# TensorE order from a list scheduler, q and k turned by DMA, and a second bank for projection two: one change to a tuned attention and MLP kernel

## The chip, the cores and the metric

The kernel runs on one core of one Trainium2 chip. The metric is the device time of one execution in microseconds, as the median of several executions. Before the change it was 508.17 us (three runs, 508.09 to 509.68). A profile gives the span of one execution, about 2 us less than its time.

Ratios below are the mean time of one kernel's fast runs over the mean of the other's fast runs of the same rounds on the same chip, so they are not quite the ratio of the medians quoted beside them. A run counts as slow when it is over 1.5% above the fastest of the same kernel.

## The reference, cut to what matters

```python
# q, k, v: (8, 12, 448, 64) float32; w_in: (768, 2048); w_out: (2048, 768); tau = 0.1
q_n = q / (norm(q, axis=-1) + 1e-6)
k_n = k / (norm(k, axis=-1) + 1e-6)
attn = softmax(q_n @ k_n.T / tau)            # per batch and head, 448 x 448
x = (attn @ v).transpose(0, 2, 1, 3).reshape(8 * 448, 768)
h = x @ w_in                                 # projection one
out = (h * cos(h)) @ w_out                   # projection two
```

## The kernel before

A **pair** is two heads of one batch; there are 48 pairs, six to a batch. A **unit** is three pairs, and there are 16 units, numbered from 0. Within a pair TensorE does this: eight transposes of the scaled q and k (into the PSUM tile TP), eight score matmuls (into SC), then for the pair before it eight matmuls of the probabilities PX with v and eight with ones, which give the row sums (both into AV). After six pairs come the 96 matmuls of projection one for a whole batch (into SC and AV again), and 112 of projection two for each batch (into PO) are spread over the following pairs as filler.

Between the attention and projection one lies a chain of small steps for each unit: DVE or ACT copies AV to xu; four DMAs gather the row sums into sums; DVE adds and inverts them (rcp); one DMA writes them to DRAM (scr); two DMAs broadcast them (RB); and POOL multiplies xu by RB into xT, the input of projection one.

The program gives every engine a fixed list of instructions. In the kernel before, a small simulation with assumed durations orders the instructions of ACT, DVE, POOL and SP. TensorE's order, after the first batch, is the order in which the program text emits it, with projection two cut into portions by hand:

```python
    def pair(g, fa, fb):
        ...
        scores(g, 0)
        scores(g, 1)
        if g >= 1 and g != PB:
            attend(g - 1, direct(g - 1))
            if g % UP == 0:
                if g > PB:
                    chain(u - 1)
                ...
        m2_fill(fa)                       # fa, fb: so many matmuls of projection two
        ...
        if g + 1 < NG and g + 1 != PB:
            transposes(g + 1)             # eight on TensorE, then a DVE copy qkT <- TP
        scores(g, 2)
        scores(g, 3)
        m2_fill(fb)

    points = {PB * (b + 1) + (4 if b == 1 else 3): b for b in range(1, B - 1)}
    for g in range(PB, NG):
        ...
        pair(g, fa, fb)
        if g in points:
            m1(points[g])                 # projection one of batch b, after pair 3 or 4 of the next batch
            m2_fill(16)
            m2_add(points[g])
```

Projection two has one PSUM bank, so each run of 16 matmuls must wait until DVE has copied the last one out (from 130 us on TensorE waited four times for this, 3.5 us in all):

```python
    PO = ps("PO", [128, 512], F32)
    banks = [[("PO", PO.ap())]]
```

Of the kernel before, what the change touches and what calls it, by code (L numbers as in the profile page):

```python
# [19 lines left out]

class Op:
    __slots__ = ("eng", "fn", "idx", "deps", "cost", "mode", "dma", "bulk", "lock", "label", "bias",
# [3 lines left out]
class Program:  # L26

# [8 lines left out]
    PATIENCE = 0.25  # L36

    def __init__(self, new_sem):
        self.new_sem = new_sem
        self.ops = []  # L40
        self.writer = {}
        self.readers = {}
        self.free = False
        self.filler = None

    def op(self, eng, fn, reads=(), writes=(), cost=0.0, mode=None, dma=None, bulk=0.0, lock=False, label="", bias=0.0):
        o = Op()
        o.eng, o.fn, o.dma, o.cost, o.mode, o.bulk, o.lock = eng, fn, dma, cost, mode, bulk, lock
        o.label, o.idx, o.inc, o.count, o.late, o.bias, o.free = label, len(self.ops), False, None, None, bias, self.free
        deps = {}  # L50
# [30 lines left out]
    def arrange(self, passes=3):  # L81
        ops = self.ops
        nominal, t = {}, 0.0
        for o in ops:
            if o.eng == "PE":
                nominal[o.idx] = t
                t += o.cost * (1.1 if o.free else 1.0)
        fixed = {o.idx: nominal[o.idx] + 8.0 for o in ops if o.free and o.eng == "PE"}
        for n in range(passes):
            late = [1e9] * len(ops)  # L90
            for o in reversed(ops):
                if o.eng == "PE":
                    late[o.idx] = min(late[o.idx], nominal[o.idx])
                if late[o.idx] > 1e8:
                    late[o.idx] = nominal[max(nominal)] + 10.0
                took = o.cost + (2.2 + o.bulk if o.dma is not None else 0.0)
                for y, _ in o.deps:
                    ty = y.cost + (2.2 + y.bulk if y.dma is not None else 0.0)
                    v = late[o.idx] - ty - self.latency(y, o)
# [4 lines left out]
            self.play()  # L104
            nominal = {o.idx: fixed.get(o.idx, o.start) for o in ops if o.eng == "PE"}
        return self

    def play(self):
        ops = self.ops
        left = [len(o.deps) for o in ops]  # L110
        ready_at = [0.0] * len(ops)
        users = [[] for _ in ops]
# [8 lines left out]
        pe = [o for o in ops if o.eng == "PE"]  # L121
        waiting = {e: [] for e in self.ENGINES}
        for o in ops:
            if left[o.idx] == 0:
                waiting[o.eng].append(o)
        todo = len(ops)
        while todo:
            best = None
            for e in self.ENGINES:
                if e == "PE":  # L130
                    s = None
                    for o in pe[: self.WINDOW if pe and pe[0].free else 1]:
                        if o.free != pe[0].free:
                            break
                        if left[o.idx] == 0:
                            t = max(free[e], ready_at[o.idx])
                            if s is None or t < s - self.PATIENCE:
                                s, c = t, (t, 0, o)
                    if s is None:
                        continue  # L140
                else:
# [4 lines left out]
                    o = min((o for o in waiting[e] if ready_at[o.idx] <= now + 1e-9), key=lambda o: (o.late, o.idx))  # L146
                    s = now
                    if o.lock and e != "SP":
                        s = max(s, port)
                    c = (s, 1, o)  # L150
                if best is None or c[:2] < best[:2]:
                    best = c
            s, _, o = best
            e = o.eng
            if e == "PE":
                pe.remove(o)
# [12 lines left out]
            if o.dma is not None:  # L169
                o.end = max(o.end + 1.7, o.start + 2.2)  # L170
                if o.bulk:
                    server = max(server, o.start + 1.2) + o.bulk
                    o.end = max(o.end, server + 1.2)
                elif server > o.start:
                    o.end += 0.8
            for w in users[o.idx]:
# [6 lines left out]
                if left[w.idx] == 0:  # L183
# [101 lines left out]
def bass_cosine_attention__then__act_gcu_kernel(  # L285
# [13 lines left out]
    UP = 3  # L299
# [10 lines left out]
    RING = 2 * S  # L310
# [541 lines left out]
```

## Time and profile before

| before | value |
|---|---|
| time | 508.17 us |
| span of the profiled run | 506.3 us |
| TensorE busy, and idle (span less busy) | 471.5 and 34.8 us |
| next busiest engine | ACT, 285.1 us |
| bytes moved by DMA | 55.42 MB |

The prediction shows the main views. The groups of instructions add the two that the change removes or reshapes. The columns are line, engine, operation, output and inputs, tiling and shapes, count, then busy time and mean duration of one in ns, then the idle time just before:

```profile
L508 PE MATMUL TP<-ident,qks 112*128 112x112 bf16 x384 | 27.9, 216 | 4.8 <-POOL qks L491 4.0 <-DVE qks L491 0.8
L539 PE MATMUL AV<-PX,va 112*64 112x448 bf16 x384 | 47.7, 368 | 4.2 <-ACT xu L565 2.2 <-DVE gT L635 1.0 <-DMA va<-in_v_dram 0.5
```

All 384 transposes run on the busiest engine, and the AV product uses column tiles of 64 where the sums use 32.

### The profile page before, as it was taken

Reading aid. Unit: us, or ns where it says so; the run is one execution under the profiler, and the core shown is the slowest. Engines: PE = TensorE matmul, PEld = TensorE weight load, DVE = VectorE, ACT = ScalarE, POOL = GpSimd, SP = SyncE. Lnnn points to the kernel's source line nnn. Section 1 sums busy time; section 2 is a strip of 40 time slices with the busy share of each in tenths; the row PEclk is TensorE's granted clock in tenths of the full one; section 3 lists DMA queues with packets and bytes.
Section 4 is the critical chain, followed back from the end, with each engine's and each line's share of the span. In section 5 each row is a group of like instructions: output and inputs, shape, how many; then the busy total and the mean of one; then the engine's idle time right before and its main releaser. Section 6 shows DMA issues by size and latency. Waiting matters only on the chain.

```text
span 506.3 us, 7822 instructions
## 1 busy us (share of the span) xinstructions
PE 471.5 (93%) x3268; PEld 226.4 (45%) x3268; DVE 223.6 (44%) x286; ACT 285.1 (56%) x347; POOL 234.3 (46%) x162
## 2 busy tenths in 40 slices
PE   8988878988999899999799999999999999999996
PEld 3333333433444445444354444444554445454553
DVE  5644544255573445435363536435343233422521
ACT  4983375877556554777237655567557654641410
POOL 4926907749977672463724864267224022002000
PEclk9999787998999999999799999999999999999999
DMA  9995692977724672186502593064501622114012
GB/s 226 178 224 141 99 236 52 209 155 195 136 60 137 156 165 56 32 170 168 114 1 86 117 220 91 5 146 113 105 6 32 120 63 54 32 35 117 1 41 85
DMA packets 51650, 55.42 MB, mean 109 GB/s; under 512 B 8864, under 2 KB 46240, under 8 KB 51616
## 3 DMA queue, kind: packets, MB, share of 16 engines
q1 hardware_dynamic: 18848, 26.61, 19.8%
q0 software_dynamic: 16256, 11.80, 16.3%
q10 hardware_dynamic: 16512, 16.52, 13.0%
q8 instruction: 26, 0.43, 0.4%
q14 instruction: 8, 0.07, 0.0%
HBM read 55.25 MB, written 11.16 MB: 131 GB/s over the span
## 4 chain that ended last, share of the span: by engine, by line
PE 59%; DMA 20%; POOL 8%; issue 5%; DVE 3%; ACT 2%; SPq 1%; POOLq 0%; ACTq 0%
PE PO L676 17%; PE SC L619 15%; DMA raw<-in_q_dram 9%; PE AV L619 8%; PE SC L525 5%; PE AV L539 5%; POOL sq L465 4%; DMA va<-in_v_dram 3%; DMA RB<-scr 3%; DMA sums<-xu 3%; PE AV L547 3%; POOL xT L605 2%; PE TP L508 2%; PE SC L676 2%; POOL qks L491 2%
## 5 line engine op out<-in xcount | busy, mean ns | idle before, releaser
L530 ACT ACTIVATE PX<-SC 112x896 bf16<-112x896 f32 x192 | 165.2, 917 | 69.7 <-PE SC L525 67.0
L676 PE MATMUL PO<-W,gT 128*128 128x384 bf16 x752 | 137.7, 330 | 3.8 <-DVE osb L688 3.5
L491 POOL TENSOR_TENSOR qks<-raw,rn 112x1024 bf16<-112x1024 f32 x47 | 88.6, 1903 | 59.4 <-ACT rn L483 46.5
L619 PE MATMUL SC<-xT,W 128*128 128x448 bf16 x480 | 100.7, 367 | 6.5 <-POOL xT L605 4.9
L676 PEld LDWEIGHTS PO<-W,gT 128*128 128x128 bf16 x752 | 68.2, 98 | 71.6 <-issue 22.1
L465 POOL TENSOR_TENSOR sq<-raw 112x1024 bf16<-112x1024 f32 x43 | 80.4, 1891 | 38.3 <-DMA raw<-in_q_dram 38.3
L605 POOL TENSOR_TENSOR xT<-xu,RB 128x448 bf16<-128x448 f32 x42 | 46.4, 1133 | 108.2 <-DMA RB<-scr 108.2
L633 ACT ACTIVATE cosb<-SC,cst 128x896 f32<-128x896 f32 x40 | 40.2, 1007 | 73.6 <-PE SC L619 73.5
L619 PEld LDWEIGHTS SC<-xT,W 128*128 128x128 bf16 x480 | 47.7, 101 | 56.2 <-issue 11.3
L472 DVE TENSOR_REDUCE n<-sq 112x16 f32<-112x1024 bf16 (+1 forms) x49 | 58.0, 1189 | 29.4 <-POOL sq L465 23.9
L525 PE MATMUL SC<-qkT 64*128 64x448 bf16 x384 | 59.7, 365 | 9.1 <-DVE qkT L516 5.2
L635 DVE TENSOR_TENSOR gT<-SC,cosb 128x896 bf16<-128x896 f32 x40 | 43.5, 1090 | 50.4 <-ACT cosb L633 50.3
L619 PE MATMUL AV<-xT,W 128*128 128x448 bf16 x288 | 58.5, 352 | 0.7
L539 PE MATMUL AV<-PX,va 112*64 112x448 bf16 x384 | 47.7, 368 | 4.2 <-ACT xu L565 2.2
L688 DVE COPY osb<-PO 128x384 f32<-128x384 f32 x47 | 25.9, 552 | 56.9 <-PE PO L676 56.7
L516 DVE COPY qkT<-TP 128x896 bf16<-128x896 bf16 x48 | 29.5, 615 | 30.9 <-PE TP L508 30.9
L633 ACT ACTIVATE cosb<-AV,cst 128x896 f32<-128x896 f32 x24 | 24.2, 1008 | 31.0 <-PE AV L619 30.0
L619 PEld LDWEIGHTS AV<-xT,W 128*128 128x128 bf16 x288 | 27.7, 98 | 28.7 <-issue 3.6
L568 DVE COPY xu<-AV 128x896 f32<-128x896 f32 x21 | 22.9, 1091 | 35.6 <-PE AV L547 35.6
L635 DVE TENSOR_TENSOR gT<-AV,cosb 128x896 bf16<-128x896 f32 x24 | 26.2, 1090 | 22.2 <-ACT cosb L633 21.9
L508 PE MATMUL TP<-ident,qks 112*128 112x112 bf16 x384 | 27.9, 216 | 4.8 <-POOL qks L491 4.0
L525 PEld LDWEIGHTS SC<-qkT 64*128 64x128 bf16 x384 | 14.4, 94 | 39.6 <-ACT PX L530 17.4
(40 smaller groups left out, 246.1 us busy)
## 6 DMA issues: line engine op xcount, KB each, us to landing
RB<-scr SPq DMA_DIRECT2D x28, 336.0 KB, 4.6
raw<-in_k_dram ACTq DMA_DIRECT2D x12, 672.0 KB, 5.9
raw<-in_q_dram ACTq DMA_DIRECT2D x12, 672.0 KB, 8.8
va<-in_v_dram POOLq DMA_DIRECT2D x16, 336.0 KB, 5.7
W<-in_moe_w_in_dram POOLq DMA_DIRECT2D x4, 768.0 KB, 13.4
W<-in_moe_w_out_dram POOLq DMA_DIRECT2D x4, 768.0 KB, 10.8
out_dram<-osb SPq DMA_DIRECT2D x8, 336.0 KB, 2.8
out_dram<-osb SPq DMA_DIRECT2D x8, 288.0 KB, 2.6
```

The source lines that it names most:

```text
L465: pool(lambda e, x=x, y=y: e.tensor_tensor(y, x, x, ALU.mult), src_, dst, 0.1 + n * 1.78e-3, label="sq%d.%d" % (u, p))
L472: dve(lambda e, w=w: e.tensor_reduce(out=n2v[i][:, 2 * p : 2 * p + 2, w], in_=sqv[p][:, :, w, :], axis=mybir.AxisListType.X, op=ALU.add), ...
L491: f = lambda e, s0=s0, s1=s1: e.tensor_tensor(qksv[i][:, s0:s1, h, :].rearrange("p s h d -> p h s d"), rawv[i][:, h, s0:s1, :], bass.AP(rn ...
L508: r = e.transpose(TP.ap()[:, NP * s : NP * s + NP], qksv[i][:, s, 2 * p : 2 * p + 2, :], ident.ap())
L525: t = e.matmul(SCv[z][:, a, 0:S], qkT[j].ap()[r, NP * c : NP * c + 128], qkT[j].ap()[r, S : 2 * S], start=True, stop=True)
L530: act(lambda e: e.activation(PXv[j][:, c], SCv[z][0:NP, :, 0:S], ACT.Exp, scale=1.0 / TAU), ["SC%d" % z], [("PX", j, c)], 2 * S, "E", labe ...
L539: t = e.matmul(AVv[64 * a : 64 * a + 64, 0, 0:S], vav[i][:, NJ * (2 * p + a) + c, :], PXv[j][:, c, a, :], start=(c == 0), stop=(c == NJ - 1))
L605: pool(lambda e, p=p: e.tensor_tensor(xTv[b % 2][:, UP * i + p, :], xuv[i][:, 0, p, :], RBv[i][:, p, :], ALU.mult), [("RB", i, p), ("xu", ...
L619: t = e.matmul(ph[:, a, 0:S], W1v[:, c, 128 * n : 128 * n + 128], xTv[b % 2][:, c, :], start=(c == 0), stop=(c == NKC - 1))
L633: act(lambda e, ph=ph, cz=cz: e.activation(cosv[cz], ph[:, :, 0:S], ACT.Sin, bias=cst.ap()[:, 0:1], scale=1.0), names(gi) + ["cst0"], [("c ...
L635: dve(lambda e, ph=ph, cz=cz, gi=gi: e.tensor_tensor(gTv[:, 2 * gi : 2 * gi + 2, S * (b % 2) : S * (b % 2) + S], ph[:, :, 0:S], cosv[cz], ...
L676: r = e.matmul(po[:, 0:HW], gTv[:, y, col : col + 128], W2v[:, y, HW * hf : HW * hf + HW], start=(y == 0), stop=(y == NF - 1))
```

## The change

Its intent is to take work off TensorE and to let it find something to do whenever one stream waits. It has four parts.

**Part 1.** From pair 10 on (number 9, counted from 0), q and k are turned by a DMA, asked for two pairs ahead, into three buffers:

```diff
     def transposes(g, apart=False):
-        u, p, j = g // UP, g % UP, g % 2
+        u, p, j = g // UP, g % UP, g % 3
+        if g >= BYPE:                              # BYPE = 9
+            dma("SP", [lambda e: e.dma_start_transpose(
+                qkT[j].ap().rearrange("p (s m) -> p s m", s=NS), qksv[i][:, p].rearrange("p s h d -> p (s h d)"))],
+                ...
+            P.ops[-1].cost = 1.2
+            return
```

**Part 2.** The AV product is cut into four column tiles of 32, the form that the sums have. (The sums of the first six pairs, 48 matmuls in tiles of 64, take that form too.)

```diff
         def av(e, c):
             for a in range(2):
-                t = e.matmul(AVv[64 * a : 64 * a + 64, 0, 0:S], vav[i][:, NJ * (2 * p + a) + c, :], PXv[j][:, c, a, :], ...)
+                for h in range(2):
+                    o = 64 * a + 32 * h
+                    t = e.matmul(AVv[o : o + 32, 0, 0:S], vav[i][:, NJ * (2 * p + a) + c, 32 * h : 32 * h + 32], ...)
```

**Part 3.** The transposes' bank becomes a second bank of projection two once the transposes on TensorE are done:

```diff
-    TP = ps("TP", [128, 1024], BF16)
+    PO2 = ps("PO2", [128, 512], F32)
+    TPv = PO2.ap().bitcast(BF16)
...
+    banks[0] = [("PO", PO.ap()), ("PO2", PO2.ap())]
```

**Part 4.** The list scheduler now chooses TensorE's order too, from two streams: the attention with projection one (A), and projection two (B). It repeats with landing times of DMAs from a model of three queues, which it takes to share the DMA engines. Weight loads at the start are chained behind one another, and projection one of a batch is offered after pair 5 of the next batch. The orders of the other engines are made anew with the same model, and one squaring step of unit 3 moves from POOL to ACT. Part 4 is thus a bundle:

```diff
+            for grp in groups[:3]:
+                t = when(grp)
+                if t is not None and (s is None or switched(t, grp[0]) < s - self.PATIENCE):
+                    s, c = switched(t, grp[0]), (t, grp[0], grp)
+            if fill and left[fill[0].idx] == 0:
+                o = fill[0]
+                t = max(free["PE"], ready_at[o.idx])
+                if s is None or switched(t, o) < s - self.HOLD:
+                    s, c = t, (t, o, fill)
...
-    points = {PB * (b + 1) + (4 if b == 1 else 3): b for b in range(1, B - 1)}
+    points = {PB * (b + 1) + 5: b for b in range(1, B - 1)}
```

## The prediction

> **What bounds the kernel now.** I read four views in this order: the page's busy line and its 40 slices, the busy time by stretch, TensorE's timeline in one steady stretch, and TensorE's own waits. The busy line and three rows of the slices come first:
>
> ```profile
> PE 471.5 (93%) x3268; PEld 226.4 (45%) x3268; DVE 223.6 (44%) x286; ACT 285.1 (56%) x347; POOL 234.3 (46%) x162
> PE   8988878988999899999799999999999999999996
> PEclk9999787998999999999799999999999999999999
> DMA  9995692977724672186502593064501622114012
> ```
>
> TensorE is the bound: 93% busy, and no other engine is above 56%. So time falls only if TensorE gets less work, fewer gaps, or fewer stretches at a low granted clock. The slices say where the weak places are: in the first quarter PE is at 8, the clock dips to 7 and 8, and the DMA row is at 9 in many slices. The windows view (columns: stretch, its length, busy time of PE, PEld, DVE, ACT and POOL, granted clock, DMA share, GB/s), cut at the start and end of the first projection (41, 68) and where the second one begins (130):
>
> ```profile
> 0.00:41.00 41.00, 35.85 (x255) 15.02 (x255) 21.78 (x32) 30.10 (x48) 21.37 (x21) 1.00 1.07 215
> 41.00:68.00 27.00, 23.09 (x111) 10.82 (x108) 15.21 (x14) 9.02 (x11) 20.54 (x14) 0.87 0.63 120
> 68.00:130.00 62.00, 51.71 (x421) 21.16 (x420) 27.36 (x38) 47.44 (x62) 40.67 (x27) 0.89 0.72 157
> 130.00:244.00 114.00, 107.17 (x768) 52.51 (x768) 55.03 (x68) 67.19 (x79) 69.45 (x45) 1.00 0.53 122
> 244.00:461.00 217.00, 214.10 (x1496) 105.20 (x1497) 90.50 (x118) 121.97 (x140) 78.92 (x55) 0.99 0.36 81
> ```
>
> From 130 us on, TensorE is nearly full at full clock; there only removed work and a few gaps can help. Before 130 us it is 111 busy of 130, 16.5 us of that is filler on the zero tile (the group PO<-zt, 68 matmuls), and from 41 to 130 the clock is 0.87 to 0.89. What one steady pair of heads costs is in the timeline (start, length, group):
>
> ```profile
> 271.61 0.56 PE L508 MATMUL TP<-ident,qks 112*128 112x112 bf16 x8
> 272.10 0.55 PE L525 MATMUL SC<-qkT 64*128 64x448 bf16 x4
> 272.58 1.47 PE L676 MATMUL PO<-W,gT 128*128 128x384 bf16 x8
> 273.99 0.66 PE L525 MATMUL SC<-qkT 64*128 64x448 bf16 x4
> 274.57 0.95 PE L539 MATMUL AV<-PX,va 112*64 112x448 bf16 x8
> 275.45 0.56 PE L547 MATMUL AV<-PX,ones 112*32 112x448 bf16 x8
> 275.95 1.47 PE L676 MATMUL PO<-W,gT 128*128 128x384 bf16 x8
> 277.26 0.56 PE L508 MATMUL TP<-ident,qks 112*128 112x112 bf16 x8
> ```
>
> Ends are modelled, so I use start to start. The eight transposes hold TensorE 272.10 - 271.61 = 0.49 us. A block of eight second-projection matmuls takes 273.99 - 272.58 = 1.41 before a block in another tiling (64*128) and 277.26 - 275.95 = 1.31 before one in the same tiling: a tiling switch costs 0.10 us. One pair is 5.65 us, of which 2.72 is projection two. TensorE's gaps from 130 us on, in the view of waits, are few:
>
> ```profile
> PE SC L619 <- POOL xT L605: 4.9, 2, 3.7
> PE PO L676 <- DVE osb L688: 3.5, 4, 1.5
> ```
>
> The 3.7 us gap is at 240.7 us, and what follows it in the timeline is dearer than it should be:
>
> ```profile
> 244.47 7.55 PE L619 MATMUL SC<-xT,W 128*128 128x448 bf16 x24 [3.72 <-POOL xT L605]
> 254.13 4.70 PE L619 MATMUL SC<-xT,W 128*128 128x448 bf16 x24
> ```
>
> The same 24 matmuls take 2.85 us more after the gap.
>
> [...] 112 x 1024 elements of 2 bytes are 0.23 MB[...]. [...] the load of q issued at 61.55 us, with weights of projection two in flight, holds 17.5 us of the chain that ended last, where the median issue to landing of such loads is 8.8.
>
> **Part 1, transposes.** Pairs 9 to 47, thus 39 of 48, get q and k turned by a DMA on the SP queue, asked for two pairs ahead, into three buffers instead of two. Removed on TensorE: 39 x 0.49 = 19.1 us, all on the bounding engine. Removed on DVE: 39 copies qkT<-TP of 0.615 us = 24 us, off the path. Added: 39 x 0.23 MB = 9 MB of DMA[...]. Two pairs of lead is about 10 us. The kernel's own cost constant for the issue is 1.2 us of SP; even if landing takes 5 us it is hidden, provided that SP isn't stuck behind another wait. The SP queue is idle mostly.
>
> **Part 2, AV in four column tiles of 32 rather than two of 64.** The number of AV matmuls doubles to 768, but four run beside each other, so array time stays. What goes is the switch between AV (112*64) and the sums (112*32): one per pair, 48 x 0.10 = 4.8 us. Risk: twice the weight loads and instructions in the same 0.88 us. The sums block already runs eight matmuls of that form in 0.50 us including a switch, so sixteen should fit in about 0.80. I count no loss.
>
> **Part 3, second bank for projection two.** The transposes' bank is free after the first nine pairs. Removes the wait on the copy osb, 3.5 us from 130 us on.
>
> **Part 4, the order.** Projection two becomes a stream that fills whenever the attention stream isn't ready, and each projection one comes after the whole of the next batch's pairs, so that its last xT has long landed. Removes from 130 us on the 3.7 us gap, the 2.85 us of low clock after it, and about 1 us before AV: 7.6 us. I charge it for finer cuts (one more switch per pair, 31 x 0.10 = 3 us) and for wrongly foreseen waits in TensorE's fixed order (I choose 7 us, some 0.2 us a pair).
>
> **From 130 us on:** 376.3 us now, minus 30 transposes blocks x 0.49 = 14.7, minus 31 x 0.10 = 3.1, minus 3.5, minus 7.6, plus 10 = 357.
>
> **Before 130 us** three bounds compete. (a) Needed TensorE work at full clock: 17 pairs x 2.44 (5.65 less 2.72 and 0.49) = 41.5, nine transposes 4.4, projection one 18.2, ten blocks of projection two 13 to 14, longer sums of the first six pairs 2.3: 80, plus about 11 before the first scores = 91. (b) DMA: the DMA view moves 21.8 MB up to 130 us; at the 215 GB/s of the first 41 us that is 101 us. (c) POOL: 82.6 us busy plus a 10 us start = 93. DMA is the highest, and it was slack for long (0.63 and 0.72 from 41 to 130). The change reorders weight loads for this: the first weights wait for the first pairs, and half of projection two's weights come before the loads of the fourth unit. I take 12 us over the highest bound: 113, a saving of 17.
>
> **Sum:** 113 + 357 = 470, minus nothing for the tail, which keeps its last 4 us. The time is 508.2 against a span of 506.3, so add 2: 472. That includes my cautious 10 us of charges; a good fit of the schedule would give 462. I predict **467 us**.
>
> **The rivals.** (1) A new wait takes the old work's place: the DMA transposes land late, because SP issues in order and stands behind a gather, a spread or an output[...]. For it: SP waits 190 us in all for the copies osb, in its own view of waits, and SP's order was drawn from a model. Against it: 10 us of lead and a third buffer. If each of 39 pairs lost 1 us, the gain of part 1 is gone twice over: 467 + 39 = 506, the same. (2) The start is held by DMA whatever the order: the first 130 us remain, less the 3 us of transposes there: 127 + 357 + 2 = 486. For it: a DMA row at 9 in the early slices, and 9 MB more traffic, though little of it early. (3) ACT becomes the bound in the pair stretches: four exps x 0.917 = 3.67, half an xu 0.46, together 4.1 us a pair against TensorE's 5.65 - 0.49 - 0.10 = 5.06. Against it: TensorE is still longer. It would show as waits of scores on exp, filled by projection two until that runs dry; perhaps 0.3 us a pair, 480. (4) The scheduler does as well as it believes and the start falls to its bound: 101 + 347 + 2 = 450.
>
> **Range and chances.** Removed work alone, 19.1 + 4.8 = 24 us, gives 484 with no gap closed; to fail a 2% gain (498) most of it would have to return as waits. Rivals 2 and 3 together make about 490, rival 4 makes 450. So 448 to 490 at 8 in 10; faster by over 2% 0.92, within 2% 0.06, slower 0.02.
>
> **What would show it right or wrong.** TP matmuls fall from 384 to 72; AV<-PX,va shows 768 in the form 112*32 and its block, with the sums, takes about 1.28 us with no switch between. PE busy falls by some 25 to 35 us, with its share at 94% or more. The wait of PO on osb vanishes. The clock stays 1.00 after 130 us. M2 blocks fill gaps of the scores. Part 1 is wrong if the waits view lists PE or PEld SC on DMA qkT for more than about 5 us; the start's step is wrong if the second projection one does not begin at least 10 us earlier for the same pairs done; part 2 is wrong if an AV block of sixteen takes over 0.9 us. The whole is wrong if TensorE's share falls below 90%, as then its fixed order met waits that the scheduler did not see.

The sum: 113 + 357 = 470 us of span, 472 of time, and the forecast of 467 lies between this and the 462 of a good fit.

What the trace of the kernel before shows: in the 7.55 us after the 3.72 us gap the granted clock was 0.61, and 1.00 where the same 24 matmuls took 4.70. That four narrow tiles run beside each other is read from start to start, less 0.10 us for the switch: a matmul of 448 columns took 0.19 us in a tile of 128 (24 in 4.54), 0.10 in tiles of 64 (8 in 0.78) and 0.05 in tiles of 32 (8 in 0.40).

## More of the kernel before

The kernel before gave medians from 505 to 509 us on the chips used here. Kernels that ran on different chips are therefore compared by their ratios to it.

## The result

The changed kernel takes **486.83 us** (median of four runs, 484.02 to 490.79), against 508.93 us (508.09 to 509.91) for the kernel before in the same rounds. The ratio is 0.960, with an interval of 0.953 to 0.967. It is faster by 4%, which is a little more than half of the 41 us predicted. Its spread from run to run is 1.4%, against 0.4% before. Two repeats on other chips gave ratios of 0.952 and 0.960.

The busy line and three of the rows of 40 slices, of the kernel after:

```profile
PE 449.3 (93%) x3395; PEld 208.9 (43%) x3395; DVE 201.2 (42%) x247; ACT 284.4 (59%) x348; POOL 232.6 (48%) x161
PE   8899968787389999999999999999999999999996
PEclk9999998898669999999999999999999999999999
DMA  8999974996936399329980899049903920150132
```

TensorE's busy time fell by 471.5 - 449.3 = 22.2 us and the span by 506.3 - 482.1 = 24.2. By this count nearly the whole gain is busy time, and idle time went only from 34.8 to 32.8 us. The 22.2 us are a net figure: the transposes lost 27.9 - 5.1 = 22.8 us of modelled busy time and projection one 4.0 us, mostly work at a low clock (before, two groups of 24 matmuls took 7.42 and 7.55 us at a granted clock of 0.62 and 0.61, and after, one took 6.49 at 0.71; at 1.00 such a group takes 4.70), while the zero-tile filler, the AV product and projection two gained some. The rows show where the idle time lies: PE falls to 3 in the slice that begins at 120.5 us, and the clock to 6 in that slice and the next. From slice 13 (144.6 us) on, PE and clock stand at 9 or more tenths, but for PE in the last slice. The windows view of the kernel after is cut at the start and end of its first projection one (about 41 and 61.5), at the start of the second (137.7), and at 244 and 461 as for the kernel before:

```profile
0.00:41.00 41.00, 37.08 (x339) 15.06 (x339) 24.25 (x34) 28.23 (x45) 27.89 (x26) 1.00 1.03 197
41.00:61.50 20.50, 20.16 (x129) 10.18 (x129) 9.48 (x10) 11.06 (x15) 8.68 (x8) 1.00 1.15 232
61.50:137.70 76.20, 54.05 (x476) 18.90 (x473) 27.93 (x34) 51.52 (x65) 44.45 (x28) 0.84 0.80 163
137.70:244.00 106.30, 105.06 (x797) 48.76 (x798) 47.85 (x57) 70.67 (x86) 72.34 (x46) 0.98 0.72 153
244.00:461.00 217.00, 216.06 (x1559) 106.00 (x1557) 87.81 (x107) 122.97 (x141) 79.19 (x56) 1.00 0.48 98
```

The first projection now runs without a gap at full clock (20.16 of 20.50 busy, clock 1.00, against 0.87 before). The stretch after it is bad: 54.05 busy of 76.20, at a clock of 0.84. After 137.7 us TensorE is full. Put as a sum, with busy time before 130 us added up from the prediction's fence:

| stretch | kernel | length | PE busy | PE idle |
|---|---|---|---|---|
| up to the second projection one | before | 130.0 | 110.7 | 19.3 |
| | after | 137.7 | 111.3 | 26.4 |
| from there to the end | before | 376.3 | 360.8 | 15.5 |
| | after | 344.4 | 338.0 | 6.4 |

The change made the start worse and the rest better. The cuts are not quite at the same work. At 137.7 us the kernel after has also done pair 17 (about 2.4 us) and 16 more matmuls of projection two (2.6 us), so at the prediction's cut its start is 137.7 - 2.4 - 2.6 = 132.7 us and its rest 349.4.

TensorE's own waits in the kernel after (what waited, for whom, us in total, times, longest):

```profile
PE AV L669 <- DVE xu L698: 9.0, 2, 6.3
PE SC L648 <- ACT PX L653: 3.4, 8, 0.8
PE PO L799 <- DVE osb L806: 3.3, 2, 3.1
PE AV L669 <- ACT PX L653: 2.8, 8, 0.4
...
PE SC L648 <- DMA qkT<-qks: 0.9, 3, 0.4
```

The wait for POOL's xT is gone, and the DMA transposes cost only 0.9 us. A wait of AV for DVE's copy xu is new. It and the osb wait sit in the bad stretch, as the timeline of TensorE there shows (start, length, group, idle before it and its releaser):

```profile
92.41 0.94 PE L669 MATMUL AV<-PX,va 112*32 112x448 bf16 x16 [2.72 <-DVE xu L698]
...
110.96 1.46 PE L799 MATMUL PO<-W,gT 128*128 128x384 bf16 x4 [3.14 <-DVE osb L806]
...
133.47 1.69 PE L669 MATMUL AV<-PX,va 112*32 112x448 bf16 x16 [6.32 <-DVE xu L698]
...
137.73 6.49 PE L749 MATMUL SC<-xT,W 128*128 128x448 bf16 x24 [0.97 <-ACT PX L653]
```

These three gaps are 12.2 us, and work after them runs slowly: the granted clock was 0.72 from 92.41 to 95.07 us, 0.53 from 110.96 to 114.30 and 0.50 from 133.47 to 137.70. The last line is 24 matmuls in 6.49 us at 0.71, where the same group takes 4.70 later, at 1.00.

Neither xu nor osb was what held DVE. Its timeline of the same stretch has the step that it stood at, in its fixed order, just before the second gap ended:

```profile
110.24 0.20 DVE L725 TENSOR_REDUCE rcp<-sums 128x21 f32<-128x42 f32 x1 [4.82 <-DMA sums<-xu]
110.36 0.55 DVE L806 COPY osb<-PO 128x384 f32<-128x384 f32 x1
```

DVE stood 4.82 us at the sum of the gathered row sums, with the osb copy that TensorE needed listed behind it. SP's queue shows when that gather was asked for, and what delayed the next steps of its chain (SPq is the issuing of DMAs):

```profile
99.73 2.52 SPq L720 DMA_DIRECT2D sums<-xu  x4
...
111.13 0.34 SPq L729 DMA_DIRECT2D scr<-rcp  x1
111.52 5.95 SPq L623 DMA_TRANSPOSE qkT<-qks  x2
117.52 1.23 SPq L731 DMA_DIRECT2D RB<-scr  x2
```

Four DMAs of 5.2 KB each were issued from 99.73 us and the sum could start at 110.24. The broadcast RB then stood behind two transposes and was issued at 117.52. The other two gaps have the same cause: their sums started at 90.9 and 130.8, some 10 us after the first DMA of each gather. Later steps of the chain are late too: POOL's multiply waited for the broadcast issued at 117.52 until 128.51, and the last xT that the second projection one needs ended at 131.8.

The view of the chain that ended last names one more late transfer in front of these. It is a bulk load of q, issued at 48.45, for which POOL stood 18.4 us:

```profile
48.45 19.66 DMA raw<-in_q_dram
```

The steady part went as hoped. A pair in the timeline of the kernel after:

```profile
272.49 0.94 PE L669 MATMUL AV<-PX,va 112*32 112x448 bf16 x16
273.26 0.55 PE L677 MATMUL AV<-PX,ones 112*32 112x448 bf16 x8
273.74 1.47 PE L799 MATMUL PO<-W,gT 128*128 128x384 bf16 x8
275.15 0.55 PE L648 MATMUL SC<-qkT 64*128 64x448 bf16 x4
275.63 1.47 PE L799 MATMUL PO<-W,gT 128*128 128x384 bf16 x8
277.04 0.66 PE L648 MATMUL SC<-qkT 64*128 64x448 bf16 x4
277.62 0.94 PE L669 MATMUL AV<-PX,va 112*32 112x448 bf16 x16
```

From AV to AV it is 277.62 - 272.49 = 5.13 us with 16 matmuls of projection two, against 5.65 before. The sixteen narrow AV matmuls hold TensorE for 273.26 - 272.49 = 0.77 us, where eight wide ones held it for 0.88. The groups confirm the counts:

```profile
L669 PE MATMUL AV<-PX,va 112*32 112x448 bf16 x768 | 48.7, 361 | 13.4 <-DVE xu L698 9.0 <-ACT PX L653 2.8 <-ACT xu L695 1.0
...
L631 PE MATMUL PO<-ident,qks 112*128 112x112 bf16 x72 | 5.1, 214 | 0.3 <-POOL qks L608 0.2
```

### The profile page after: what moved, and what is told of

Same layout as the page of the kernel before. It is cut to its first block, busy times and chain, and to the rows that moved or that the text cites. A ratio compares the mean times of both kernels' runs of the same rounds, so it can differ in the third digit from the quotient of the medians.

```text
span 482.1 us, 8113 instructions
## 1 busy us (share of the span) xinstructions
PE 449.3 (93%) x3395; PEld 208.9 (43%) x3395; DVE 201.2 (42%) x247; ACT 284.4 (59%) x348; POOL 232.6 (48%) x161
## 3 DMA queue, kind: packets, MB, share of 16 engines
q1 hardware_dynamic: 55040, 35.56, 34.1%
## 4 chain that ended last, share of the span: by engine, by line
PE 66%; DMA 16%; ACT 11%; POOL 2%; SPq 2%; DVE 1%; issue 1%; ACTq 0%; POOLq 0%
PE PO L799 21%; PE SC L749 17%; PE AV L749 10%; ACT PX L653 7%; DMA sums<-xu 6%; PE SC L648 6%; PE AV L669 5%; DMA raw<-in_q_dram 4%; DMA W<-in_moe_w_out_dram 3%; DMA qkT<-qks 2%; PE AV L677 2%; PE SC L799 2%; PE PO L834 2%; ACT L521 1%; SPq L720 1%; DMA scr<-rcp 1%
## 5 line engine op out<-in xcount | busy, mean ns | idle before, releaser
L799 PE MATMUL PO<-W,gT 128*128 128x384 bf16 x816 | 149.8, 331 | 5.0 <-DVE osb L806 3.3
L799 PEld LDWEIGHTS PO<-W,gT 128*128 128x128 bf16 x816 | 74.0, 98 | 76.6 <-issue 27.6
L749 PE MATMUL SC<-xT,W 128*128 128x448 bf16 x480 | 96.7, 357 | 1.2 <-ACT PX L653 1.0
L582 POOL TENSOR_TENSOR sq<-raw 112x1024 bf16<-112x1024 f32 x42 | 78.6, 1893 | 25.0 <-DMA raw<-in_q_dram 21.5
L806 DVE COPY osb<-PO 128x384 f32<-128x384 f32 x51 | 28.2, 552 | 102.8 <-PE PO L799 102.8
L589 DVE TENSOR_REDUCE n<-sq 112x16 f32<-112x1024 bf16 (+1 forms) x49 | 57.9, 1189 | 19.8 <-POOL sq L582 13.4
L669 PE MATMUL AV<-PX,va 112*32 112x448 bf16 x768 | 48.7, 361 | 13.4 <-DVE xu L698 9.0
L561 POOL DMA_DIRECT2D va<-in_v_dram x16 | 13.0, 815 | 62.5 <-PE AV L669 51.3
L763 ACT ACTIVATE cosb<-AV,cst 128x896 f32<-128x896 f32 x24 | 24.2, 1007 | 31.3 <-PE AV L749 31.2
L765 DVE TENSOR_TENSOR gT<-AV,cosb 128x896 bf16<-128x896 f32 x24 | 26.2, 1091 | 19.9 <-ACT cosb L763 19.3
L698 DVE COPY xu<-AV 128x896 f32<-128x896 f32 x21 | 22.7, 1083 | 25.5 <-PE AV L677 22.8
L669 PEld LDWEIGHTS AV<-PX,va 112*32 112x32 bf16 x768 | 16.3, 96 | 37.9 <-issue 11.8
```

Of the source, the lines that this page charges most:

```text
L582: pool(lambda e, x=x, y=y: e.tensor_tensor(y, x, x, ALU.mult), src_, dst, 0.1 + n * 1.78e-3, label="sq%d.%d" % (u, p))
L589: dve(lambda e, w=w: e.tensor_reduce(out=n2v[i][:, 2 * p : 2 * p + 2, w], in_=sqv[p][:, :, w, :], axis=mybir.AxisListType.X, op=ALU.add), ...
L669: t = e.matmul(AVv[o : o + 32, 0, 0:S], vav[i][:, NJ * (2 * p + a) + c, 32 * h : 32 * h + 32], PXv[j][:, c, a, :], start=(c == 0), stop=(c ...
L749: t = e.matmul(ph[:, a, 0:S], W1v[:, c, 128 * n : 128 * n + 128], xTv[b % 2][:, c, :], start=(c == 0), stop=(c == NKC - 1))
L763: act(lambda e, ph=ph, cz=cz: e.activation(cosv[cz], ph[:, :, 0:S], ACT.Sin, bias=cst.ap()[:, 0:1], scale=1.0), names(gi) + ["cst0"], [("c ...
L765: dve(lambda e, ph=ph, cz=cz, gi=gi: e.tensor_tensor(gTv[:, 2 * gi : 2 * gi + 2, S * (b % 2) : S * (b % 2) + S], ph[:, :, 0:S], cosv[cz], ...
```

## The experiments

Sixteen runs were made, each with three timed rounds beside the kernel before. In the table, idle is the span less TensorE's busy time of the profiled run. One of these profiled runs was slow (marked), so its span is not compared with the others.

| kernel | median us | ratio | span | PE busy | idle |
|---|---|---|---|---|---|
| before | 508.93 | 1 | 506.3 | 471.5 | 34.8 |
| before + part 1 | 508.94 | 1.001 | 509.5 | 457.9 | 51.6 |
| before + parts 1, 2 | 509.49 | 1.002 | 506.5 | 452.7 | 53.8 |
| before + parts 1, 2, 3 | 506.04 | 0.993 | 502.7 | 450.4 | 52.3 |
| part 4 with part 2 alone | 517.73 | 1.023 | 514.8 | 468.4 | 46.4 |
| after without part 3 | 521.43 | 1.028 | 526.9 (slow) | 462.1 | 64.8 |
| after without part 2 | 491.15 | 0.966 | 490.5 | 457.7 | 32.8 |
| after | 486.83 | 0.960 | 482.1 | 449.3 | 32.8 |

The texts name their theories by letters. A and B concern the start: late gathers at which DVE stands in its order (A1 late through bulk loads, A2 through the transposes' bytes), or the sheer length of the chain (B). C and D concern the parts: removed work that pays by itself (C), or a second bank worth more than its old wait (D).

### Which part makes the gain

**before_turns** is the kernel before with part 1 alone, and **before_both** with parts 1 and 2. TensorE's order stays as written by hand.

```diff
 # before_turns, on the kernel before; before_both also has the AV edit of part 2
-    qkT = sbs("qkT", 2, [128, 2 * S], BF16)
+    qkT = sbs("qkT", 3, [128, 2 * S], BF16)
...
+        if g >= BYPE:
+            dma("SP", [lambda e: e.dma_start_transpose(...)], ...)
...
-        if g + 1 < NG and g + 1 != PB:
+        if g + 1 < BYPE and g + 1 != PB:
             transposes(g + 1)
+        if BYPE <= g + 2 < NG:
+            transposes(g + 2)
```

> The kernel before with one part of the change alone: q and k of pairs 9 on turned by DMA on the SP queue two pairs ahead, three buffers, TensorE's order as written by hand. If what the whole change gained is just the removed work (the order's gain and loss cancel), the 39 blocks of 0.49 us, less what the start keeps as waits, give 12 to 18 us: ratio 0.965 to 0.976. If the DMA transposes carry a wait of their own that the hand-written order can't fill, it gains under 6 us.

> The kernel before with two parts of the change alone: the DMA transposes and the AV products in four column tiles of 32, TensorE's order as written by hand, one bank for projection two. Theory C (the list order and the second bank gave nothing net: what they took from the gaps after 130 us was lost again before 138 us): ratio 0.955 to 0.967, as the whole change. Against it, that the order carries a good half of the gain: ratio above 0.972.

Measured: 508.94 us (ratio 1.001, interval 0.996 to 1.007) and 509.49 us (1.002, 0.996 to 1.008). Busy time fell by 13.6 and 18.8 us, and the time did not move. Both forecasts of a gain are missed: 12 to 18 us for part 1 alone, and theory C's ratio of 0.955 to 0.967 for both. Waits for DMA transposes, the other explanation, don't appear in either list. In TensorE's waits of before_turns the larger part of the work came back as these:

```profile
PE SC L625 <- POOL xT L611: 11.6, 3, 9.6
PE PO L682 <- DVE osb L694: 7.7, 17, 2.8
```

They were 4.9 and 3.5 us in the kernel before. Pairs that finish sooner reach projection one before its chain has delivered xT, and reach the next run of projection two before its bank is empty. Removed work alone gives nothing in a fixed order that was fitted to the old work.

**hand_bank** adds part 3 to before_both, so it has all but part 4. **hand_late** is the same with projection one placed later, as the changed kernel places it. **changed_third** is the control on that chip.

```diff
 # hand_bank, on before_both
-    TP = ps("TP", [128, 1024], BF16)
+    PO2 = ps("PO2", [128, 512], F32)
+    TPv = PO2.ap().bitcast(BF16)
...
     m2_add(0)
+    banks[0] = [("PO", PO.ap()), ("PO2", PO2.ap())]
...
 # hand_late, on hand_bank
-    points = {PB * (b + 1) + (4 if b == 1 else 3): b for b in range(1, B - 1)}
+    points = {PB * (b + 1) + 5: b for b in range(1, B - 1)}
```

> The kernel before with the transposes of pairs 10 on by DMA, the AV product in column tiles of 32, and the second bank for projection two in alternation, in the order written by hand, no list scheduler for TensorE. Theory O (the list order is what turns the removed work into time): 500 to 510, as with the two parts alone, with the waits of scores for POOL's xT of about 11 us still there. Theory B (the second bank is what does it, the order adds little): 480 to 492, with projection two's wait for DVE's osb copies (7.2 us in the run with the two parts alone) down to under 2 us. Between 492 and 500 both have a share.

> As hand_bank, with projection one of each later batch one or two pairs later (after pair 5 of the next batch, where the changed kernel's program also offers it). Theory L (what kept the removed work from paying was that projection one stood before the end of the chain gather, sums, broadcast, xT): the wait for POOL's xT falls from 11 to under 3 us, and the time is 8 to 12 us under hand_bank. Theory O: it changes under 4 us, since the gaps reappear elsewhere in a fixed order. If it comes under 484 it beats both kernels.

> The changed kernel without an edit, as the control on this chip: 484 to 489, ratio 0.952 to 0.962 to the kernel before.

Measured: hand_bank 506.04 us (0.993, 0.985 to 1.002), hand_late 510.29 us (1.001, 0.991 to 1.010), changed_third 487.63 us (0.960). Theory O stands: with three of the four parts the time is within 1% of the kernel before, and part 4 is worth about 18 us on top. TensorE's waits in hand_bank:

```profile
PE SC L628 <- POOL xT L614: 16.4, 5, 6.5
PE SC L532 <- ACT PX L537: 8.2, 19, 1.4
PE AV L548 <- ACT xu L574: 6.3, 3, 5.9
```

The second bank did its task there, since no wait for osb is left in the list (7.2 us in before_both), but the wait for xT grew by about as much. In hand_late the wait for xT is gone and scores wait 21.8 us for DMA transposes instead. Its profiled run was slow, so that number is only an indication. Theory L foresaw rightly that the wait for xT would go, but the 8 to 12 us that it expected from this did not come: moving one thing in an order written by hand moved the gap.

**one_bank** is the changed kernel without part 3, and **all_pe** also without part 1; both are rescheduled by the list scheduler.

```diff
 # one_bank; all_pe also sets BYPE = 48, so that every transpose stays on TensorE
-    banks[0] = [("PO", PO.ap()), ("PO2", PO2.ap())]
```

> The changed kernel with the second bank of projection two taken away (all halves accumulate in the first one until the end), schedule made anew. My prediction gave the bank 3.5 us: then 3 to 6 us slower than the changed kernel, 487 to 492, ratio 0.957 to 0.967. Rival D (the list order fills TensorE with runs of projection two, and a run longer than one half of 16 matmuls must wait for the copy out of a single bank of about 0.9 us; so the bank is what lets the order fill): 10 to 22 us slower, 495 to 507, with many waits of PO on osb.

> The changed kernel with all transposes on TensorE again, which also takes away the second bank (the transposes need it); the list order and the AV form stay. If the list order carries the gain by itself, the time is the changed kernel's plus the removed 19 us of transposes, 503 to 508, or less. If order, bank and DMA transposes need one another (each alone gains nothing): the time is that of one_bank plus about 15 to 19 us, so no better than the kernel before: 505 to 525, ratio 0.995 to 1.03.

Measured: 521.43 us (1.028, 1.021 to 1.034) and 517.73 us (1.023, 1.019 to 1.028). Both are slower than the kernel before (for all_pe the interval straddles the 2% line). All_pe lies in the range of the second theory, but not by its sum: it is 4 us below one_bank and not 15 to 19 above it. The profiled run of one_bank was slow, but all its runs were above 516 us. TensorE's waits in it begin with these:

```profile
PE PO L799 <- DVE osb L806: 19.9, 25, 6.3
PE AV L669 <- DVE xu L698: 15.3, 4, 6.7
```

Where projection two runs beside nothing else, each run of 16 is followed by one of these waits, as its timeline shows:

```profile
451.15 2.77 PE L799 MATMUL PO<-W,gT 128*128 128x384 bf16 x16 [0.65 <-DVE osb L806]
454.65 2.77 PE L799 MATMUL PO<-W,gT 128*128 128x384 bf16 x16 [0.72 <-DVE osb L806]
```

From start to start that is 3.50 us, where runs of 16 in alternating banks start 2.60 us apart in the kernel before (448.11, 450.72 and 453.32 us): about 0.9 us more for each run. So the list order puts runs of projection two back to back, and with one bank that costs more than it gains. Removing the bank costs (1.028 - 0.958) x 505 = some 35 us, with 0.958 as the mean of the three ratios of the changed kernel. That is ten times the 3.5 us predicted for it, and more than any theory gave it (rival D: 10 to 22 us). It isn't all due to the bank's own wait: that wait grew from 3.3 to 19.9 us, and the new order has other waits too (xu, 15.3 us). A new order can by itself cost some 20 us, as bype18 shows below, so what the bank alone is worth in the list order is not separated. In the order by hand the bank gave 1.002 - 0.993 = 0.9%, 4.5 us, with intervals that overlap.

**av64** undoes part 2 alone, with every engine's order kept. **changed_again** is the control on the same chip.

```diff
-                for h in range(2):
-                    o = 64 * a + 32 * h
-                    t = e.matmul(AVv[o : o + 32, 0, 0:S], vav[i][:, NJ * (2 * p + a) + c, 32 * h : 32 * h + 32], ...)
+                t = e.matmul(AVv[64 * a : 64 * a + 64, 0, 0:S], vav[i][:, NJ * (2 * p + a) + c, :], PXv[j][:, c, a, :], ...)
```

> The changed kernel, every order unchanged, with the AV products back in two column tiles of 64 (384 instructions in place of 768), so that the switch of tiling between AV and the sums returns. The prediction's 0.10 us per pair: from 138 us on 31 pairs x 0.10 = 3 us longer, some of the rest hidden in the start: 3 to 5 us slower than the control. The rival, that 16 instructions of 32 columns cost more to issue than 8 of 64: the same as the control or faster.

> The changed kernel unaltered, as a control on the chip of the next three runs: time within 478 to 491 us, ratio to the kernel before 0.95 to 0.97. It is also what the spread from run to run is read from: two earlier rounds gave 484 to 491.

Measured: 491.15 us against 485.48 for the control, 5.7 us more (ratios 0.966 and 0.952). That is a little over the 3 to 5 us expected, and within the spread it is what the prediction's count of switches gave part 2, 4.8 us (4.2 by a right count, as shown below). The control's ratio has an interval of 0.945 to 0.960, and its gaps at the start are those of the kernel after (1.5, 4.6 and 6.5 us), so these belong to the order and not to one execution.

### Where the start's gain went

**dve_swap** moves only DVE's sum and reciprocal of units 2, 3 and 4 behind the copies that TensorE waited for.

```diff
+    sums_, recs_ = ([o for o in P.ops if o.label == n] for n in ("sum", "recip"))
+    def put(u, behind):
+        for n, o in enumerate((sums_[u - 2], recs_[u - 2], find("spread%d" % u))):
+            o.start = max(o.start, behind.start + 1e-3 * (n + 1))
+    put(2, find("xu9"))
+    put(3, [o for o in P.ops if o.label == "osb2"][0])
+    put(4, find("xu15"))
```

> The changed kernel with only the vector engine's order touched: in three places the small sum and reciprocal of a chain (which wait for the gathered sums) go behind the copy that they stood ahead of (xu of pair 9, osb of tile 2, xu of pair 15). TensorE's, ScalarE's and GpSimd's orders are unchanged. Theory A (TensorE's three gaps of 2.7, 3.1 and 6.3 us before the second projection one come from VectorE standing in order behind a late gather, and its low clock comes from those gaps): the waits of AV on xu and of PO on osb before 138 us fall from 12.2 to under 2 us, and the time falls by at least 6 us, to 471 to 480. Theory B (the start is held by the chain gather, spread, broadcast, xT anyway, which gives its last xT at about 132 us): the same gaps move into a wait for xT in front of the second projection one, and the time falls by 0 to 6 us, to 481 to 487.

Measured: 485.56 us (0.958, 0.950 to 0.965), the same as the changed kernel within the intervals, so theory A's 471 to 480 was missed. The time lies in theory B's 481 to 487, but B's sign, a wait for xT in front of the second projection one, did not show. The profiled run was slow, so its sizes are only indications: AV's wait for xu fell from 9.0 to 2.7 us, but scores waited 8.7 us for DMA transposes, 3.75 of it at 97.7 us, and xu of pair 15 waited for POOL. DVE's order was the place where the lateness showed, not its cause.

**light_loads** and **light_turns** give wrong results (relative errors 0.65 and 0.52). All orders stay; only bytes go. The first cuts the loads of q, k and v of units 4 to 7 to one head of six, the second the DMA transposes of pairs 9 to 17 to a seventh.

```diff
 # light_loads
-        h = slice(2 * p0, 2 * p1)
+        few = 1 if u in (4, 5, 6, 7) else 2 * (p1 - p0)
 # light_turns
-        u, p, j = g // UP, g % UP, g % 3
+        u, p, j, n = g // UP, g % UP, g % 3, 16 if g < 18 else NP
```

> The changed kernel, every order unchanged, but the loads of q, k and v of units 4 to 7 move one head of six (the result is wrong on purpose). Theory A1 (the gathers of the early stage are late because these bulk loads share the DMA engines): the gathers of units 2 to 4 land in about 4 us instead of 8 to 10 from the first issue, TensorE's three gaps before the second projection one vanish, and the time falls by 12 to 20 us, to 466 to 474. Theory A2 (the gathers are late because they stand behind the DMA transposes in SP's own ring): the landing stays at 7 us or more, and the time falls by under 5 us.

> The changed kernel, every order unchanged, but the nine DMA transposes of pairs 9 to 17 turn 16 partitions of 112, a seventh of the bytes (the result is wrong on purpose). Theory A2 (the transposes clog SP's ring in front of the gathers): the gathers of units 2 to 4 land in about 4 us, the gaps before the second projection one shrink by more than half, and the time falls by 8 to 18 us, to 468 to 478. Theory A1 (bulk loads are the cause): the gathers still take 7 us or more and the time falls by under 4 us.

Measured: 477.52 us (0.944, 0.938 to 0.950) and 480.29 us (0.952, 0.946 to 0.958). There was no control of the changed kernel on this chip. In light_loads the second projection one starts at 127.40 us instead of 137.73, and AV waits 1.5 us for xu. The view of the tile sums gives the time from issue to landing of the gathers, minimum, median and maximum. Over the whole run it is this, first the kernel after, then light_loads:

```profile
DMA to landing us min/median/max: 1.9/5.3/10.8
```

```profile
DMA to landing us min/median/max: 1.9/3.2/10.3
```

The bulk loads of later units are not cut, so the stretch from 75 us to the second projection one says more; again the kernel after, then light_loads:

```profile
DMA to landing us min/median/max: 7.2/8.0/9.3
```

```profile
DMA to landing us min/median/max: 2.0/2.3/4.0
```

The kernel before has a median of 4.9 us there, and light_turns 6.9. In light_turns the sums still start 8.6 to 11.0 us after the first DMA of their gathers, the second projection one starts at 134.24, and a wait of 7.03 us for xu is there. So bulk loads beside the gathers make them late (8.0 us, and 2.3 without most of their bytes), and the bytes of the transposes do so little (6.9 with a seventh of them). Theory A1 was right on the landing, but its time of 466 to 474 us was missed. By the ratios, light_loads gains (0.958 - 0.944) x 505 = 7 us on the mean of the three ratios of the changed kernel; by the profiled runs it is 482.1 - 470.9 = 11. The interval of light_loads overlaps with that of one of the three.

**bype18** keeps the transposes on TensorE through pair 17, so that the DMA queue is free of them at the start. The order is made anew. There is a second difference: up to pair 17 the transposes and projection two now share the bank PO2.

```diff
-    BYPE = 9
+    BYPE = 18
```

> The changed kernel with the transposes of pairs 9 to 17 given back to TensorE (DMA from pair 18 on), and the schedule made anew with that. TensorE gains 9 blocks of 0.49 us, 4.4 us, in the stage in which it idles anyway; VectorE 9 copies of 0.6. Theory A2 (early DMA transposes are what makes the start late): the time falls by 5 to 15 us, to 471 to 481. Theory A1 or B: the same within 4 us or slower by up to 5, 483 to 492.

Measured: 506.19 us (1.003, 0.998 to 1.008). Every expectation was missed. TensorE is 453.4 us busy and 50.1 idle: scores wait 8.2 us for the DVE copy qkT at 71 us, AV 8.4 us for xu at 246 us, and scores 9.7 us for a DMA transpose at 303 us. It says nothing on the start's cause. It shows that a new order from the same model can give back the whole gain.

### Tries at a better version

**hold67** holds bulk loads of units 6 and 7 until the gather, or the broadcast, of unit 3 has landed. **told234b** holds nothing and tells the scheduler that the gathers of units 2, 3 and 4 take 5.5, 2.5 and 5 us longer than its model says. **told_turn25** tells it also that every DMA transpose lands 2.5 us later.

```diff
 # hold67
+    for u, x in ((6, "gather3"), (7, "bcast3")):
+        after(last_of("load u%d p0" % u), last_of(x))
+        after(last_of("load v u%d" % (u - 1)), last_of(x))
 # told234b
+    MORE = {'gather2': 5.5, 'gather3': 2.5, 'gather4': 5.0}
...
+        more = self.MORE.get(o.label, 0.0)
 # told_turn25, in place of the line above
+        more = self.MORE.get(o.label, 0.0) + (2.5 if o.label[0] == "T" else 0.0)
```

> An attempt at a better kernel and a test of theory A1 without wrong results: the bulk loads of unit 6 (with v of 5) wait until the gather of unit 3 has landed, those of unit 7 (with v of 6) until the broadcast of unit 3 has; schedule made anew. Theory A1: the gather of unit 3 takes about 5 us instead of 10 from its first issue, the broadcast of unit 3 lands within 6 us instead of 10, the second projection one starts at 127 to 132 us rather than 138 to 140, and the time is 474 to 480. If the loads only come late elsewhere in exchange: 482 to 490.

> An attempt at a better kernel: the scheduler is told the landing times that the trace showed for the gathers of units 2 to 4 (5.5, 2.5 and 5 us more than it reckoned), nothing else changes but the order that follows. If the loss of the start is the scheduler's wrong time for the gathers (VectorE's order places a wait ahead of copies that TensorE needs): the waits of AV on xu and PO on osb before 140 us fall under 4 us and the time is 472 to 480. If the start is held by the length of the chain itself: 480 to 486, the gaps moving to another wait.

> The changed kernel with a scheduler that is told that the gathers of units 2, 3 and 4 take 5.5, 2.5 and 5 us longer and that every DMA transpose lands 2.5 us later than its queue model says. Theory M (both losses are orders made from landing times that are too early): second projection one starts at 128 to 131 us, scores wait for DMA transposes under 2 us in sum (5.5 us without the margin), and the time is 474 to 481. Theory F (any fixed order meets new waits, and a margin only moves them): 484 to 492. Its own model gives a span 2.9 us longer than that of the changed kernel.

Measured: 497.80 us (0.984), 489.66 us (0.964, 0.957 to 0.971) and 500.37 us (0.983, 0.974 to 0.991). None beats the changed kernel, and all three missed the times expected of them. In hold67 the twelve gathers up to the second projection one landed in 2.7 us (median), as theory A1 has it and with right results. But that projection still started at 133.29 us, and scores waited 13.8 us in all for DMA transposes. In told234b the second projection one started at 129.88 us, so the start gained 8 us. From there to the end it took 352.8 us instead of 344.4, with these among TensorE's waits:

```profile
PE SC L650 <- DMA qkT<-qks: 5.5, 4, 3.1
```

In told_turn25 the margin still left 3.7 us of that wait, the second projection one started at 136.26 us, and other waits came, two of which the timeline shows well after the start:

```profile
188.42 1.22 PE L671 MATMUL AV<-PX,va 112*32 112x448 bf16 x16 [3.90 <-DVE xu L700]
...
249.20 1.69 PE L671 MATMUL AV<-PX,va 112*32 112x448 bf16 x16 [6.71 <-DVE xu L700]
```

Theory F of that run stands, and even its 484 to 492 was too low. The scheduler's own model expected spans of 471.9 us for the changed kernel and 474.8 for told_turn25 (it works them out when the program is built). The profiles gave 482.1 and 499.8. The model is thus off by 10 to 25 us, in an amount that it doesn't foresee, and that is as much as the differences that it is asked to decide.

## Why the prediction was wrong in size and right in kind

**What bounds the kernel: right over the whole span.** TensorE was and is the busiest engine by far, at 93% in both.

**Parts 1 and 2: right, as removed work.** The sum of 24 us of removed work was 22.2 us of busy time in the profile, and undoing part 2 alone cost 5.7 us against 4.8 predicted. The sign that was named for part 1 to be wrong, scores waiting over 5 us for DMA transposes, did not show in the changed kernel (0.9 us on its matmuls, 3.5 on its weight loads), although it did in several reordered ones. The count of 48 switches was wrong by six: in the first six pairs AV and sums were both in tiles of 64, so 42 x 0.10 = 4.2 us. Busy time was to fall by 25 to 35 us, which the net 22.2 misses. A DMA transpose took about 1.65 us of all DMA engines, an estimate worked out in the last section; the author's own estimate, now cut, was lower.

**From 130 us on: better than predicted.** The step gave 357 us and the kernel took 349.4 at the same cut. Of the charges of 10 us little came. The steady pair took 5.13 us where the removals alone give 5.65 - 0.49 - 0.10 = 5.06, so finer cuts cost about 0.07 us a pair in place of 0.10, and idle time fell to 6.4 us.

**Before 130 us: this is the step that failed.** It was "I take 12 us over the highest bound: 113, a saving of 17". At the same cut the start took 132.7 us, so the saving was less than nothing, and the sign named for this came: the second projection one did not begin 10 us earlier. Two terms of the step were wrong. The first is the highest bound, DMA, which used the traffic of the kernel before. The windows view up to the second projection one shows it, first before, then after:

```profile
0.00:130.00 130.00, 110.66 (x780) 47.01 (x781) 64.34 (x84) 86.55 (x120) 82.58 (x62) 0.92 0.81 168
0.00:137.70 137.70, 111.30 (x939) 44.14 (x939) 61.65 (x77) 90.81 (x123) 81.02 (x60) 0.91 0.92 183
```

The kernel after moved 183 GB/s x 137.7 us = 25.2 MB by then, not 21.8, and the DMA share rose from 0.81 to 0.92. At the step's own 215 GB/s that is 117 us in place of 101, as an estimate; some of these loads could have come later.

The second is the 12 us above the bound. The three bounds (TensorE, DMA bytes, POOL) were each a sum of work, and none held the chain of latencies that the trace shows: gather, sum, spread, broadcast, xT. Its small DMAs landed late beside bulk loads (the gathers in 8.0 us, and in 2.3 with the loads cut), with DVE, and behind it TensorE, standing in a fixed order. Cutting the bulk loads of units 4 to 7 brought the second projection one to 127.4 us and left only one gap above 1 us in front of it (1.5 us for xu). So these loads account for some 10 of the missing 17 to 20 us (7 us in the timed ratios). That run takes away the bytes and what they do to the gathers together, and hold67, with early gathers but a new order, started at 133.29; how much is bytes and how much is latency is therefore not shown. The rest is argued only. In the stretch up to 130 us the filler of projection two runs dry at about 117 us, and scores then wait up to 0.8 us at a time for exp, as rival 3 said of the pair stretches. The late load of q (19.66 us) was touched by no run.

**Part 3: right in sign, mis-sized.** The step read the bank's worth off the wait on osb in the kernel before, 3.5 us. In the order by hand that is about what the bank gave (4.5 us, not resolved). In the list order its removal cost some 35 us, of which 19.9 - 3.3 = 16.6 us stand as waits on osb between long runs of projection two (in a slow profiled run) and the rest came with the new order.

**Part 4 as 7.6 us of closed gaps: wrong as a way of counting.** The parts are not a sum. With three parts and the order by hand the gain was 0.7%; with the list order and no second bank, a loss of 2 to 3%; with all, a gain of 4 to 5%. The 24 us of removed work turned into time only because part 4 and the bank kept idle time from growing: 52.3 us idle with the hand order, 32.8 with the list order, at the same busy time within 1.1 us. The sentence "removed work alone, 24 us, gives 484 with no gap closed" was therefore right for the changed kernel by two errors that cancel. Removed work alone gave nothing, and the start lost about what the rest gained over it. That was luck.

**The rivals.** Rival 2, the first 130 us unchanged and 486 us in all, is what came in time. Its reason is at least half right: DMA did hold the start, with the latency of small transfers in it and not only bytes. (The 3 us of transposes that it takes off are 9 x 0.49 = 4.4.) Rival 1, SP's order in the way, shows in a broadcast behind two transposes for 6 us. Rival 3 shows in small waits on exp (3.4 and 2.8 us), and rival 4 did not come.

**What stays open.** Which piece of part 4 makes its 18 us: TensorE's list order, the model of landing times, the order of the loads or the orders of the other engines. And whether a schedule exists that keeps the start's 8 to 10 us and the quiet rest as well. Three tries at it were slower than the changed kernel or no faster, because each change of the order met other late DMAs.

## What to carry to other kernels

Before work taken off the busiest engine is counted as time, ask who is ready to fill the space. In a fixed order fitted to the old work, 19 us of removed work became 19 us of waiting, and only a new schedule with the buffers that it needs turned it into time. A bound for a start-up stretch must include its longest chain of small steps, with each small DMA timed as it lands beside bulk loads and not alone (here 8.0 and 2.3 us). The worth of a buffer read off its present wait holds only for the present order.

## What the traces show of the hardware

- DMA transposes: the queue that carries them took 34.1% of 482.1 us after and 19.8% of 506.3 us before. The difference of 64.2 us over 39 transposes of 0.23 MB is 1.65 us each, about 140 GB/s, as an estimate: it takes all of the difference to be theirs, though other packets on that queue may have slowed too. Their time to landing was 2.6, 5.5 and 12.2 us as minimum, median and maximum. Issuing one took SP 1.25 us in the median and 4.2 at most. The line of that queue, first before and then after (packets, MB, share of 16 engines):

```profile
q1 hardware_dynamic: 18848, 26.61, 19.8%
```

```profile
q1 hardware_dynamic: 55040, 35.56, 34.1%
```

- Small transfers beside bulk loads: gathers of 5.2 KB landed in 1.9 us at best, in 8.0 us (median) at the start of the kernel after, and in 2.3 us there with the bulk loads cut.
- A change of tiling on TensorE: 0.10 us here, as the difference of two start-to-start times. Sixteen matmuls in column tiles of 32 took no longer than eight in tiles of 64 (0.77 us with no switch after them, and 0.88 with one).
- Slow work after a gap: after one of 2.49 us in hand_bank, preceded by steady work, 24 matmuls took 6.18 us where 4.70 is normal, thus at 0.76 of the normal rate. After a longer gap later in the same run they took 4.70, so the length of the gap alone does not tell:

```profile
187.53 6.18 PE L628 MATMUL SC<-xT,W 128*128 128x448 bf16 x24 [2.49 <-POOL xT L614]
304.79 4.70 PE L628 MATMUL SC<-xT,W 128*128 128x448 bf16 x24 [3.30 <-POOL xT L614]
```
